# Earlier loads and transposes for the seventh pair, and third products spread one block per pass

## The chip, the cores and the metric

The kernel runs on one core of one Trainium2 chip. The metric is device time of one execution in microseconds (us). A profiled execution gives a span, from the first to the last instruction; it is usually 1.7 to 2.0 us shorter than the time. A single-core run is called slow when it is over 1.5% above the fastest of the same kernel; only fast runs are compared.

Engines in the profile: PE is TensorE (PEld its weight loads), DVE is VectorE, ACT is ScalarE, POOL is GpSimd, SP is SyncE. `L330` is line 330 of that run's own source, so line numbers shift a little between kernels.

## The reference, cut to what matters

```python
def reference(q, k, v, lam, moe_w_q, moe_w_k, moe_w_out):      # batch 4, 8 heads, 768 tokens, 64 columns
    x = linear_attention(q, k, v, lam)      # causal, decayed by lam per head, a running state per head
    x = x.transpose(0, 2, 1, 3).reshape(4, 768, 512)
    wq, wk = x @ w_q, x @ w_k               # 512 -> 64
    W = einsum('bsd,btd->bst', wq, wk) / 8
    mixed = einsum('bst,btd->bsd', W, x)
    return maximum(mixed, 0) @ w_out
```

The kernel uses that `W @ x` is `wq @ (wk.T @ x)`: a small product Y = wk.T x, then the "third products" Y.T wq (tile pm, evicted with Relu to rmT), then the output products with w_out (tile po).

## The kernel before

There are 16 pairs of heads (4 batches of 4 pairs) and one pass of the main loop for each, counted from 0. Pass n computes the scores of pair n, finishes pair n-1 and transposes q and k of pair n+1. Batch b's four pairs are complete about one pass after its last; the products for its 768 outputs are strewn over the passes of the next batch. The parts that matter, cut:

```python
    load_q(5); load_kv(5, "k"); load_wqk(); load_kv(5, "v")          # all on GpSimd's DMA queue
    nc.gpsimd.dma_start(out=wo, in_=moe_w_out...)                    # output weights, 512 KB in bf16
    pool = {0: ["q6", "s4", "k6", "v6"], 1: ["q7", "s5", "k7", "v7"], ...}   # s: scaling of v, on GpSimd
    for n in range(N):
        ...                                                          # GpSimd: what pool has for pass n
        outs      = {6: [(0, 0)], 9: [(0, 4)], 12: [(1, 0)], 13: [(1, 2)], 14: [(1, 3)], 15: [(1, 5)]}
        late_outs = {6: [(0, 1)], 7: [(0, 2)], 8: [(0, 3)], 10: [(0, 5)], 12: [(1, 1)], 14: [(1, 4)]}
        if n > 9 and n % 4 in (3, 0):
            mix_pm((n - 5) // 4, [0, 1] if n % 4 == 3 else [2, 3], engs=(nc.scalar, nc.vector) * 2)
        scores(n)
        inter(n - 1)                         # sums of states of pair n-1, times q
        masks(n, ((0, 0), (0, 1)))           # VectorE, PSUM -> SBUF
        back()                               # values(n-1), flip(n-2), mix_po for outs, in pass 9 and 13 mix_wk
        masks(n, ((1, 0),));  turn_q(n + 1)  # not in pass 5
        masks(n, ((1, 1),));  turn_k(n + 1)  # not in pass 5
        if n == 5: mix_wq(0); mix_py(0)
        states(n)
        for i, t in late_outs: mix_po(i, t)  # of pass n
        sums(n)
        if n == 5:
            mix_pm(0, [0, 1], ...); mix_pm(0, [2, 3], ...)
            turn(n + 1)
        if n in (9, 13): mix_wq(p); mix_py(p)
```

`mix_py` makes Y: twelve matmuls into PSUM, then three copies on ScalarE, all of which have to be done before the second matmul of a third-product block can start:

```python
        nc.scalar.copy(out=Y[:, 0, :], in_=py)
        for i in range(2):                                  # the same with its halves swapped
            nc.scalar.copy(out=Y[i * 64 : i * 64 + 64, 1, :], in_=py[o, :])
```

`mix_pm(b, [dd])` is one block: two matmuls of 384 columns and two evictions of 128x384, one on ScalarE and one on VectorE. The program hands out eight banks of PSUM (the memory that matmuls write to); a tile's bank is free when its eviction, the copy of it to SBUF, is done.

Of the kernel before, what the change touches and what calls it, by code (L numbers as in the profile page):

```python
# [28 lines left out]
def kernel(  # L29
# [11 lines left out]
    nc = tc.nc  # L41
# [16 lines left out]
    def pst(shape, dt, name):  # L58
        i = free.pop(0)
        t = ps.tile(shape, dt, tag=f"p{i}", name=name)  # L60
        held[id(t)] = (t, i)
        return t
# [5 lines left out]
    N = len(pairs)  # L68
# [4 lines left out]
    def q_rows(n):  # L73
        b, kk = pairs[n]
        return q[b, 2 * kk : 2 * kk + 2].rearrange("h (a p r) d -> p h a (r d)", p=128, r=2)

    def kv_rows(n, src):
        b, kk = pairs[n]
        return src[b, 2 * kk : 2 * kk + 2].rearrange("h (c p) d -> p h c d", p=128)

    def load_q(n):
        t = stage.tile([128, 2, 3, 2 * D], BF16, tag="fq", name="fq")
        nc.gpsimd.dma_start(out=t, in_=q_rows(n))  # L83
        staged[n, "q"] = t

    def load_kv(n, nm):
        t = stage.tile([128, 2, NCH, D], BF16, tag="f" + nm, name="f" + nm)
        nc.gpsimd.dma_start(out=t, in_=kv_rows(n, dict(k=k, v=v)[nm]))  # L88
        staged[n, nm] = t
# [137 lines left out]
    def turn(n):  # L227
        turn_q(n)
        turn_k(n)

    def turn_q(n):
        b, kk = pairs[n]
        fq = staged.pop((n, "q"))
        trq = pst([128, NCH, 2, 64], BF16, "trq")
        for a in range(3):
            for r in range(2):
                for hl in range(2):
                    nc.tensor.transpose(  # L238
                        trq[hl * 64 : hl * 64 + 64, 2 * a : 2 * a + 2, r, :],
                        fq[:, hl, a, r * D : (r + 1) * D],  # L240
                        ident,
                    )
        qT = tsb.tile([128, S], BF16, tag="qT", name="qT")
        nc.vector.tensor_tensor(  # L244
            out=qT,
            in0=trq.rearrange("d c r p -> d (c r p)"),
            in1=Dq[kk],
            op=ALU.mult,
        )
        done(trq)  # L250
        L[n]["qT"] = qT
# [75 lines left out]
    def masks(n, which):  # L327
        for a, hl in which:
            t = prb.tile([128, 3, CH], BF16, tag="pr", name="pr")
            nc.vector.tensor_tensor(out=t, in0=L[n]["sc"][a, hl], in1=maskc, op=ALU.mult)  # L330
            done(L[n]["sc"][a, hl])
            L[n]["pr"][a, hl] = t
# [83 lines left out]
    def mix_wq(b, kts=range(NP)):  # L416
        if 0 in kts:
            M[b]["wq"] = pst([128, HALF], F32, "wq")
        wq = M[b]["wq"]
        for kt in kts:  # L420
            for n in range(2):
                nc.tensor.matmul(  # L422
                    wq[n * 64 : n * 64 + 64, :],
                    wqk[:, 0, kt, :],
                    xT[b][:, kt, n * HALF : (n + 1) * HALF],
                    start=(kt == 0),
                    stop=(kt == NP - 1),
                    skip_group_check=True,
                )
        if NP - 1 in kts:  # L430
            wqT = hyp.tile([128, HALF], BF16, tag="wqT", name="wqT")
            nc.scalar.copy(
                out=wqT.rearrange("j (c p r) -> j c r p", c=3, r=2),
                in_=wq.rearrange("j (c r p) -> j c r p", c=3, r=2),
            )
            done(wq)
            M[b]["wqT"] = wqT
# [25 lines left out]
    def mix_pm(b, which, wide=True, engs=None):  # L463

        if isinstance(which[0], int):
            which = [(dd, n) for dd in which for n in range(2)]
        pms = [pst([128, HALF], F32, "pm") for _ in which]
        for m in range(1 if wide else 2):
            for (dd, n), pm in zip(which, pms):
                r = slice(n * 64, n * 64 + 64)  # L470
                c = (dd % 2) * CH
                if wide:
                    o, w = slice(0, 128), slice(c, c + CH)
                else:
                    o, w = slice(m * 64, m * 64 + 64), slice(c + m * 64, c + m * 64 + 64)
                nc.tensor.matmul(  # L476
                    pm[o, :],
                    M[b]["Y"][r, int(dd // 2 != n), w],
                    M[b]["wqT"][r, :],
                    start=True,  # L480
                    stop=True,
                    skip_group_check=True,
                )
        for i, ((dd, n), pm) in enumerate(zip(which, pms)):
            to = M[b]["rmT"][:, dd, n * HALF : (n + 1) * HALF]
            if engs and engs[i] is nc.vector:
                nc.vector.tensor_scalar(  # L487
                    out=to,
                    in0=pm,
                    scalar1=1.0 / 8.0,  # L490
                    scalar2=0.0,
                    op0=ALU.mult,
                    op1=ALU.max,
                )
            else:
                nc.scalar.activation(out=to, in_=pm, func=ACT.Relu, scale=1.0 / 8.0)  # L496
            done(pm)
# [10 lines left out]
    def mix_po(b, t, last=False):  # L508
# [39 lines left out]
    load_kv(5, "k")  # L548
    load_wqk()
    load_kv(5, "v")  # L550
    nc.gpsimd.dma_start(
        out=wo, in_=moe_w_out.rearrange("(kt p) (a j) -> p a kt j", p=128, j=CH)
    )


    pool = {
        0: ["q6", "s4", "k6", "v6"],
        1: ["q7", "s5", "k7", "v7"],
        2: ["q8", "k8", "s6", "v8"],
        3: ["q9", "s7", "k9", "v9"],  # L560
        4: ["q10", "s8", "k10", "v10"],
    }
    for n in range(N):
        b, kk = pairs[n]
        for what in pool.get(n, []):
            if what[0] == "s":
                scale_v(int(what[1:]), nc.gpsimd)
            elif what[0] == "q":
                load_q(int(what[1:]))
            else:  # L570
                load_kv(int(what[1:]), what[0])
        if 11 <= n + 5 < N:
            load_more(n + 5)
        if n + 5 >= N and n + 3 < N:
            scale_v(n + 3, nc.gpsimd)
        if n == 9:

            late = consts.tile([1, D], BF16, name="late")
            nc.sync.dma_start(out=late, in_=staged[14, "v"][0:1, 0, 0, :])
            store()  # L580
        p = b - 1
        outs = {
            6: [(0, 0)],
            9: [(0, 4)],
            12: [(1, 0)],
            13: [(1, 2)],
            14: [(1, 3)],
            15: [(1, 5)],
        }.get(n, [])

        late_outs = {
            6: [(0, 1)],
            7: [(0, 2)],
            8: [(0, 3)],
            10: [(0, 5)],
            12: [(1, 1)],
            14: [(1, 4)],
        }.get(n, [])

        def back():  # L600

            if kk == 1 and n > 8:
                flip(n - 2, nc.scalar)
            if n >= 1:
                values(n - 1)
            if n >= 2 and not (kk == 1 and n > 8) and n != 5:
                flip(n - 2, nc.scalar if n < 5 else None)
            for i, t in outs:
                mix_po(i, t)
            if kk == 1 and n > 8:  # L610
                mix_wk(p)


        if n > 9 and n % 4 in (3, 0):
            mix_pm(
                (n - 5) // 4,
                [0, 1] if n % 4 == 3 else [2, 3],
                engs=(nc.scalar, nc.vector) * 2,
            )
        scores(n)  # L620
        if n >= 1:
            inter(n - 1)
        masks(n, ((0, 0), (0, 1)))
        back()

        if 1 <= n < 3:
            make_dq(n + 1)
        if n in (2, 3):
            scale_v(n, nc.vector)
        masks(n, ((1, 0),))  # L630
        if n < N - 1 and n != 5:
            turn_q(n + 1)
        masks(n, ((1, 1),))
        if n < N - 1 and n != 5:
            turn_k(n + 1)
        if n == 5:

            mix_wq(p)
            mix_py(p)
        states(n)  # L640
        if n == 4:
            flip(n - 1)
        for i, t in late_outs:
            mix_po(i, t)
        sums(n)
        if n == 0:
            scale_v(1, nc.vector)
        if n == 4:
            mix_wk(p, (0, 1, 2))
            mix_wk(p, (3,))  # L650
        if n == 5:
            for dds in ([0, 1], [2, 3]):
                mix_pm(0, dds, engs=(nc.scalar, nc.vector) * 2)
            turn(n + 1)
        if kk == 1 and n > 8:
            mix_wq(p)
            mix_py(p)
# [53 lines left out]
```

## Time and profile before

| | before |
|---|---|
| time, median of 4 runs | 99.84 us (99.44 to 100.2) |
| span of the profiled run | 97.8 us |
| scores of passes 5, 6, 9, 10, 13, 14 start at | 27.59, 34.20, 46.00, 51.44, 64.22, 69.65 us |
| last inter products (pair 15) start at | 78.08 us |

### The profile page before, as it was taken

The page shows a single profiled execution, that of the slowest core. Times are in us where ns is not written, and L with a number is a line of the kernel's source. Part 1 is how long each engine was busy: PE and PEld are TensorE (multiplying, and loading weights), DVE is VectorE, ACT ScalarE, POOL GpSimd, SP SyncE. Part 2 cuts the span into 40 slices and gives each one's busy share as a digit, 9 for nine tenths or more (in the row PEclk, how much of TensorE's full clock was granted, in tenths as well). Part 3 has the DMA queues.
Part 4 walks back from the last instruction along what each step waited for, and adds up shares of the span by engine and source line. Part 5 has one row for each costly group of instructions (what it writes and reads, how often), then busy time and mean ns, then how long its engine had stood idle before and what let it go on. Part 6 is the DMA issues. An engine that isn't in the chain of part 4 may idle for free.

```text
span 97.8 us, 3522 instructions
## 1 busy us (share of the span) xinstructions
PE 84.5 (86%) x1507; PEld 56.7 (58%) x1507; DVE 71.0 (73%) x156; ACT 62.0 (63%) x118; POOL 66.7 (68%) x69
## 2 busy tenths in 40 slices
PE   4997578598997599999999997999999999999940
PEld 1344466377875376866788475668865466433420
DVE  6648978799685986998389999974989971283520
ACT  5084477976939846664768864667977746677230
POOL 5999999999999598999999999998050000000000
PEclk9999999999999999999999999999999999999999
DMA  0999999999999999999999999999999224325583
GB/s 9 220 160 157 167 165 160 166 165 158 171 184 156 166 168 158 158 146 130 139 160 163 131 151 133 128 156 187 290 401 371 97 107 184 137 111 210 215 316 113
DMA packets 68976, 16.79 MB, mean 172 GB/s; under 512 B 65762, under 2 KB 66018, under 8 KB 68962
## 3 DMA queue, kind: packets, MB, share of 16 engines
q0 software_dynamic: 63776, 9.90, 139.0%
q1 hardware_dynamic: 5042, 6.56, 18.7%
q8 instruction: 11, 0.18, 0.7%
q10 hardware_dynamic: 144, 0.13, 0.4%
q14 instruction: 3, 0.02, 0.1%
HBM read 20.19 MB, written 6.29 MB: 271 GB/s over the span
## 4 chain that ended last, share of the span: by engine, by line
PE 36%; POOL 29%; DMA 13%; DVE 12%; issue 3%; ACT 3%; POOLq 0%
PE po L515 16%; DMA fv<-in_v_dram 8%; POOL fv L88 7%; POOL fk L88 7%; POOL fq L83 6%; DMA fk<-in_k_dram 6%; DVE pr L330 5%; POOL vn L212 4%; PE xp L379 3%; PE oa L359 3%; DVE rmT L487 2%; PE wk L402 2%; PE py L443 2%; PE wq L422 2%; PE trk L258 2%
## 5 line engine op out<-in xcount | busy, mean ns | idle before, releaser
L330 DVE TENSOR_TENSOR pr<-sc,maskc 128x384 bf16<-128x384 f32 x64 | 33.3, 550 | 2.1 <-PE sc L317 1.8
L515 PE MATMUL po<-wo,rmT 128*128 128x512 bf16 (+1 forms) x100 | 24.0, 372 | 0.0
L212 POOL TENSOR_TENSOR vn<-fv,DvI 128x768 bf16<-128x768 bf16 x12 | 18.2, 1514 | 4.1 <-PE oa L359 2.7
L371 ACT CAST xnat<-oa 128x384 bf16<-128x384 f32 x31 | 13.4, 483 | 8.7 <-PE oa L359 8.7
L527 ACT COPY osb<-po 128x512 f32<-128x512 f32 (+1 forms) x22 | 12.6, 579 | 9.7 <-PE po L515 9.7
L262 ACT COPY kT<-trk 128x768 bf16<-128x768 bf16 x16 | 12.8, 799 | 7.3 <-PE trk L258 7.2
L88 POOL DMA_DIRECT2D fv<-in_v_dram x16 | 17.1, 1069 | 0.0
L88 POOL DMA_DIRECT2D fk<-in_k_dram x15 | 16.1, 1075 | 0.0
L83 POOL DMA_DIRECT2D fq<-in_q_dram x16 | 14.2, 885 | 0.8 <-POOLq L695 0.8
L515 PEld LDWEIGHTS <-rmT 128*128 128x128 bf16 x100 | 8.5, 98 | 8.4 <-issue 0.8
L317 PE MATMUL sc<-qT,kT 64*128 64x128 bf16 x192 | 8.9, 218 | 4.2 <-ACT kT L262 2.4
L244 DVE TENSOR_TENSOR qT<-trq,dq 128x768 bf16<-128x768 bf16 x16 | 8.8, 553 | 4.2 <-PE trq L238 2.7
L317 PEld LDWEIGHTS <-kT 64*128 64x128 bf16 x192 | 5.9, 94 | 8.6 <-ACT kT L262 6.5
L258 PE MATMUL trk<-ident,fk 128*64 128x128 bf16 x180 | 7.7, 221 | 2.3 <-DMA fk<-in_k_dram 2.2
L238 PE MATMUL trq<-ident,fq 128*64 128x128 bf16 x192 | 8.5, 224 | 0.2 <-DMA fq<-in_q_dram 0.2
L487 DVE TENSOR_SCALAR rmT<-pm 128x384 bf16<-128x384 f32 x16 | 8.1, 550 | 0.6 <-PE pm L476 0.6
L359 PE MATMUL oa<-vn,pr 128*128 128x64 bf16 x192 | 8.4, 194 | 0.0
L379 PE MATMUL xp<-ident,xnat 128*128 128x128 bf16 x96 | 8.0, 220 | 0.2
L238 PEld LDWEIGHTS <-fq 128*64 128x64 bf16 x192 | 5.9, 110 | 3.3 <-issue 2.0
L277 PE MATMUL dps<-vn,fk 128*64 128x128 bf16 (+4 forms) x150 | 7.6, 232 | 0.1
L258 PEld LDWEIGHTS <-fk 128*64 128x64 bf16 x180 | 5.7, 110 | 3.3 <-DMA fk<-in_k_dram 3.3
L496 ACT ACTIVATE rmT<-pm 128x384 bf16<-128x384 f32 x16 | 7.0, 496 | 0.1
(62 smaller groups left out, 112.7 us busy)
## 6 DMA issues: line engine op xcount, KB each, us to landing
out_dram<-osb SPq DMA_DIRECT2D x23, 256.0 KB, 2.7
fq<-in_q_dram POOLq DMA_DIRECT2D x16, 192.0 KB, 5.7
fv<-in_v_dram POOLq DMA_DIRECT2D x16, 192.0 KB, 5.7
fk<-in_k_dram POOLq DMA_DIRECT2D x15, 192.0 KB, 6.0
wo<-in_moe_w_out_dram POOLq DMA_DIRECT2D x1, 512.0 KB, 9.4
k<-in_k_dram SPq DMA_DIRECT2D x1, 384.0 KB, 3.7
out_dram<-osb ACTq DMA_DIRECT2D x1, 128.0 KB, 2.1
out_dram<-osb SPq DMA_DIRECT2D x1, 128.0 KB, 2.1
```

Of the source, the lines that this page charges most:

```text
L83: nc.gpsimd.dma_start(out=t, in_=q_rows(n))
L88: nc.gpsimd.dma_start(out=t, in_=kv_rows(n, dict(k=k, v=v)[nm]))
L212: eng.tensor_tensor(out=vn, in0=fv, in1=DvI[:, 2 * kk : 2 * kk + 2, :].unsqueeze(3).to_broadcast([128, 2, NCH, D]), op=ALU.mult,)
L238: nc.tensor.transpose(trq[hl * 64 : hl * 64 + 64, 2 * a : 2 * a + 2, r, :], fq[:, hl, a, r * D : (r + 1) * D], ident,)
L258: nc.tensor.transpose(trk[hl * 64 : hl * 64 + 64, c * CH : (c + 1) * CH], kn[:, hl, c, :], ident)
L262: nc.scalar.copy(out=kT, in_=trk)
L317: nc.tensor.matmul(sc[a, hl][:, cc, :], kT[r, c * CH : (c + 1) * CH], qchunk(n, r, c), start=True, stop=True, skip_group_check=True,)
L330: nc.vector.tensor_tensor(out=t, in0=L[n]["sc"][a, hl], in1=maskc, op=ALU.mult)
L359: nc.tensor.matmul(oa[hl][:, c, :], pr[c // 3, hl][:, c % 3, :], vn[:, hl, c, :], start=False, stop=(c == NCH - 1), skip_group_check=True,)
L371: nc.scalar.copy(out=to, in_=oa[hl])
L515: nc.tensor.matmul(po, M[b]["rmT"][:, kt, t * CH : (t + 1) * CH], wo[:, c // CH : (c + w) // CH, kt, :], start=(kt == 0), stop=(kt == 3),)
L527: nc.scalar.copy(out=osb[:, c : c + w], in_=po.rearrange("p a j -> p (a j)"))
```

## The change

It wants to fill the hole of pass 5 by transposing pair 6 before the third products of batch 0, which needs q and k of pair 6 to be loaded ahead of the output weights. It also spreads the third products of batches 0, 1 and 2 over the passes, one block of a batch at a time, ahead of the scores, so that VectorE never has four evictions or two at once to do. As the blocks end later, the output products move to later passes. The last batch's third products stay where they are. The diff, cut to its core:

```diff
     load_kv(5, "v")
+    load_q(6)
+    load_kv(6, "k")
     nc.gpsimd.dma_start(out=wo, ...)
-        0: ["q6", "s4", "k6", "v6"],
+        0: ["s4", "v6"],
+    thirds = {7: [(0, 2)], 8: [(0, 3)], 10: [(1, 0)], 11: [(1, 1)], 12: [(1, 2)],
+              13: [(1, 3)], 14: [(2, 0)], 15: [(2, 1)]}
-        outs:      6: [(0, 0)], 9: [(0, 4)], 12: [(1, 0)], 13: [(1, 2)], 14: [(1, 3)], 15: [(1, 5)]
+        outs:      8: [(0, 0)], 10: [(0, 3)], 13: [(1, 0)], 14: [(1, 2)], 15: [(1, 4)]
-        late_outs: 6: [(0, 1)], 7: [(0, 2)], 8: [(0, 3)], 10: [(0, 5)], 12: [(1, 1)], 14: [(1, 4)]
+        late_outs: 8: [(0, 1)], 9: [(0, 2)], 10: [(0, 4)], 12: [(0, 5)], 13: [(1, 1)], 14: [(1, 3)], 15: [(1, 5)]
-        if n > 9 and n % 4 in (3, 0):
-            mix_pm((n - 5) // 4, [0, 1] if n % 4 == 3 else [2, 3], engs=(nc.scalar, nc.vector) * 2)
+        for i, dd in thirds.get(n, []):
+            mix_pm(i, [dd], engs=(nc.scalar, nc.vector))
         scores(n)
...
-        if n < N - 1 and n != 5:
+        if n < N - 1:
             turn_q(n + 1)
+        if n == 5:
+            mix_wq(p)
         masks(n, ((1, 1),))
-        if n < N - 1 and n != 5:
+        if n < N - 1:
             turn_k(n + 1)
         if n == 5:
-            mix_wq(p)
             mix_py(p)
...
         if n == 5:
-            for dds in ([0, 1], [2, 3]):
-                mix_pm(0, dds, engs=(nc.scalar, nc.vector) * 2)
-            turn(n + 1)
+            mix_pm(0, [0, 1], engs=(nc.scalar, nc.vector) * 2)
```

More of the change, by code (lines that the diff above doesn't have):

```diff
@@ L561 @@
         4: ["q10", "s8", "k10", "v10"],
+    }
+    thirds = {
+        7: [(0, 2)],
+        8: [(0, 3)],
+        10: [(1, 0)],
+        11: [(1, 1)],
+        12: [(1, 2)],
+        13: [(1, 3)],
+        14: [(2, 0)],
+        15: [(2, 1)],
     }
@@ L582 @@
         outs = {
-            6: [(0, 0)],
-            9: [(0, 4)],
-            12: [(1, 0)],
-            13: [(1, 2)],
+            8: [(0, 0)],
+            10: [(0, 3)],
+            13: [(1, 0)],
+            14: [(1, 2)],
+            15: [(1, 4)],
+        }.get(n, [])
+        late_outs = {
+            8: [(0, 1)],
+            9: [(0, 2)],
+            10: [(0, 4)],
+            12: [(0, 5)],
+            13: [(1, 1)],
             14: [(1, 3)],
             15: [(1, 5)],
-        }.get(n, [])
-        late_outs = {
-            6: [(0, 1)],
-            7: [(0, 2)],
-            8: [(0, 3)],
-            10: [(0, 5)],
-            12: [(1, 1)],
-            14: [(1, 4)],
         }.get(n, [])
@@ L611, in back @@
                 mix_wk(p)
-        if n > 9 and n % 4 in (3, 0):
-            mix_pm(
-                (n - 5) // 4,
-                [0, 1] if n % 4 == 3 else [2, 3],
-                engs=(nc.scalar, nc.vector) * 2,
-            )
+        for i, dd in thirds.get(n, []):
+            mix_pm(i, [dd], engs=(nc.scalar, nc.vector))
         scores(n)
```

## The prediction

> **What bounds the kernel now.** One core, 99.59 us; the profiled execution spans 97.8 us, so about 1.8 us lie outside the span and I take them as constant. Passes of the main loop are counted from 0 as in the code: pass n scores pair n and transposes q and k of pair n+1. I read the page's busy shares first.
>
> ```profile
> PE 84.5 (86%) x1507; PEld 56.7 (58%) x1507; DVE 71.0 (73%) x156; ACT 62.0 (63%) x118; POOL 66.7 (68%) x69
> ```
>
> No engine is full over the span, so the limit changes by stage and an average decides nothing. Next the chain of waits in order of time (start, length, what):
>
> ```profile
> 27.01 1.50 POOL vn L212
> 28.51 0.98 POOL fk L88
> 29.49 7.49 DMA fv<-in_v_dram
> 36.98 0.07 issue
> 37.05 0.33 POOL vn L212
> ...
> 38.47 5.65 DMA fk<-in_k_dram
> 44.12 0.04 issue
> 44.16 0.53 PE trk L258 x12
> 44.69 0.41 PE dps L277 x10
> 45.10 0.98 PE po L515 x4
> ```
>
> The reader is to see that until 44.12 us the end is set by the loads alone: GpSimd issues, v of pair 7 lands at 36.98, its scaling on GpSimd follows, only then is k of pair 9 issued, and it lands at 44.12. TensorE enters the chain there. From then on the chain is TensorE, with VectorE between 52.9 and 60.3 and again between 74.3 and 78.0.
>
> Then the timeline of PE (start, length, line, operation) around the places where the change acts:
>
> ```profile
> 29.30 0.82 PE L443 MATMUL py<-xnat,wkn 128*64 128x256 bf16 x12
> 29.96 0.58 PE L277 MATMUL dps<-vn,fk 128*64 128x320 bf16 x10
> 30.59 0.33 PE L476 MATMUL pm<-wqT,Y 64*128 64x384 bf16 x1
> 31.36 0.82 PE L476 MATMUL pm<-wqT,Y 64*128 64x384 bf16 x7 [0.43 <-ACT Y L458]
> 32.11 0.53 PE L238 MATMUL trq<-ident,fq 128*64 128x128 bf16 x12
> 32.65 0.53 PE L258 MATMUL trk<-ident,fk 128*64 128x128 bf16 x12
> 34.20 0.51 PE L317 MATMUL sc<-qT,kT 64*128 64x128 bf16 x12 [1.03 <-DVE qT L244]
> ...
> 50.68 0.82 PE L443 MATMUL py<-xnat,wkn 128*64 128x256 bf16 x12
> 51.44 0.51 PE L317 MATMUL sc<-qT,kT 64*128 64x128 bf16 x12
> ```
>
> Two readings. Pass 5 has a hole: third products (pm) wait for Y, the pair-6 transposes stand behind them, and scores of pass 6 start at 34.20 after 1.03 us idle. And a pm placed right after py cannot start: py starts at 29.30, the pm that needs all of Y at 31.36, 2.06 us later. In pass 9 py starts at 50.68 and scores follow 0.76 us later, because there the pm comes one pass later. ACT's timeline has the cause, three copies one after the other:
>
> ```profile
> 51.55 0.37 ACT L452 CAST Y<-py 128x256 bf16<-128x256 f32 x1
> 51.93 0.74 ACT L458 CAST Y<-py 64x256 bf16<-64x256 f32 x2
> ```
>
> Y is complete at 52.67, 1.99 us after py began.
>
> **What the Trainium skill says.** (1) "PSUM — Partial Sum Buffer", section "Engine vs sequencer instructions": matmuls start and complete in program order. The trace agrees: q of pair 6 landed at 31.28, but its transposes ran at 32.11, behind the waiting pm. So a waiting pm ahead of scores holds the scores. (2) "TensorE: Matmul & The Clock Gate", "Back-to-back issue gap": N/2.4 + 2.5 ns, 216 ns for 512 columns. The chain has a four-matmul output product (po) at 0.86 us, 215 ns each: agrees; 0.97 us where the chain counts the last one's drain. (3) "DMA: Bandwidth & Descriptors", "Anatomy of one DMA": about 2.0 us plus bytes/436e3, 2.45 us for 192 KB. The trace differs: k of pair 9, with a short queue, took 5.65 us; I use that. (4) "Perfetto Trace Analysis", "Optimization Strategy": the most contended engine can change over time; the trace agrees, as above.
>
> **The change part by part.** Nothing is added or removed: same matmuls, evictions and transfers, in another order.
>
> *Loads.* Issues were v5, wo, q6, scaling of v4, k6, v6; they become v5, q6, k6, wo, scaling, v6. Landings of the trace: v5 26.92, wo 29.75 (2.83 later), q6 31.28, k6 32.60, v6 33.37. At about 1.3 us each q6 should land near 28.3, k6 near 29.6, wo near 32.4; v6 and all after it as before, since the sum of work ahead is the same. Hence v7 at 36.98 and k9 at 44.12 stay: neither waits for TensorE. The scaling of v4 ends about 1.2 us later, near 25.3, still before its use at 25.63.
>
> *Pass 5.* Pair 6's q is turned from 28.63 (0.46), wq 0.67, k turned near 29.75 (0.36), py from 30.15, dps, four pm at about 32.3, scores of pass 6 near 32.7: 1.5 us earlier than 34.20.
>
> *Passes 6 to 8.* Before, four po ran here, after only two (passes 6 and 7 have none). But transposes need k7 (35.84), k8 (39.68) and k9 (44.12). Pass 7's scores come near 37.1 (before 38.62), pass 8's near 40.95 (before 42.17), and in pass 8 the k transposes wait for k9 until 44.12 (before: same). Then dps and one po as before: scores of pass 9 at about 46.0, before 46.00. The gain is zero there, and two po (0.86 + 0.97 = 1.83 us of TensorE) that before were done are still to do.
>
> *Pass 9.* First-factor products (wk) come straight after values instead of behind a po, so they stall on ACT's copy of the last transpose (ends 48.08), and end near 48.7 (before 49.1): -0.35. One late po: +0.97. Then pm(1,0) right after py: scores at py + 2.2 instead of + 0.76: +1.45. Scores of pass 10: 51.44 + 2.1 = 53.5.
>
> *Passes 10 to 12.* Pass 10 gets two po instead of one, +0.86, less two pm: pass 11 starts at 58.0 against 55.18, +2.8. Passes 11 and 12 were bound by VectorE, with two evictions of pm (0.47 each) at the head of each: before 55.40 to 59.71, 4.31 each. With one, 3.85 each, from 58.1: 62.0 and 65.85. The state sums that end there release the inter products of pass 13, at 66.0 against 64.56: +1.4. So about 1.4 us come back, 0.9 of it the two evictions moved into TensorE-bound passes, the rest gaps that VectorE had before in pass 12. po that filled this VectorE-bound stretch (two in pass 12, now one) went to passes where TensorE sets the pace.
>
> *Pass 13.* Two po instead of one, +0.97; pm(2,0) behind py again, +1.45: scores of pass 14 at 73.5 against 69.65, +3.85.
>
> *Passes 14 and 15.* Pass 14: two fewer pm, -0.15. Pass 15: before, 74.26 to 78.08 was set by VectorE with about 0.35 us of slack on TensorE; with a second po (0.9) TensorE sets it, +0.55. At the last inter products: 78.08 + 4.25.
>
> *Tail.* From there the code is the same, 19.6 us.
>
> Check by another sum: 1.83 (two po behind the k9 gate) + 2 x 1.27 (idle for Y) + 0.4 (wk stall) - 0.5 (balance of VectorE relief and lost filling) = 4.3 us. I chose 4.0, since a hand-made sum forgets small slack more often than it invents it: 99.6 + 4.0 = 103.6 us.
>
> **The rivals.** (a) *The hole of pass 5 is worth its whole size*: 1.5 us are gained and stay, giving 98.1 us. For it: the hole is real, 1.03 us idle plus the Y wait. Against it: the chain runs through v7, its scaling and k9 at that time, not through TensorE. (b) *Levelling wins*: one VectorE eviction per pass instead of two relieves passes 11 and 12, and po moved there costs nothing; with the Y wait hidden the sum would be 4.25 - 2.9 = +1.3 us, 100.9 us, or even 99.6 if the two po also fell into slack. For it: VectorE is the chain in 52.9 to 60.3. Against: py to complete Y is 1.99 us both times it can be read, and nothing stands between py and pm in the new order. (c) *The loads shift*: if q6 and k6 ahead of wo let GpSimd run ahead and k9 lands 0.5 us earlier, all gains 0.5 us: 103.1; if wo or a full set of eight outstanding loads holds GpSimd up, k9 lands later and it is 104 or more. The trace shows eight completion semaphores in turn on GpSimd's loads, and k6 would have to wait for 21.31 and wo for 22.37, within 0.2 us of when they would be issued anyway.
>
> **Range and chances.** Low end 102.0: half of the Y stall or one of the two po is absorbed and k9 is a little early. High end 104.8: no relief in passes 11 and 12. Within 2% means below 101.6 us; that needs both Y stalls hidden, which I give 0.09. Faster by over 2% needs rival (a) and more: 0.02. Slower by over 2%: 0.89.
>
> **What would show it.** Right: scores of pass 6 near 32.7; k9's landing still near 44.1 with TensorE idle before it in passes 6 to 8; scores of pass 9 near 46.0; a wait of PE on ACT's Y of about 1.2 us in passes 9 to 10 and 13 to 14; VectorE no longer taking two evictions of pm together in passes 11 and 12; a tail of 19.6 us. Wrong: k9 clearly before 43.5; scores of pass 9 before 45; no wait of pm on Y; or passes 10 to 12 shorter than 11.5 us from scores to scores.

## More of the kernel before

The busy shares of the whole span, the chain of waits and the timeline around the changed places are shown in the prediction. What they don't show is how full each engine is stage by stage. The following view of the kernel before gives the busy time of each engine in stretches: pass 5, passes 6 to 8, pass 9, passes 10 to 12, pass 13, passes 14 to the last inter products, and the tail. Columns: stretch, its length, then busy us (and instructions) of PE, PEld, DVE, ACT, POOL, the granted clock, DMA share and GB/s.

```profile
27.59:34.20 6.61, 5.08 (x99) 3.71 (x97) 5.32 (x11) 5.05 (x11) 5.52 (x6) 1.00 2.15 168
34.20:46.00 11.80, 11.71 (x238) 8.29 (x237) 10.21 (x21) 6.73 (x12) 11.52 (x12) 1.00 2.09 153
46.00:51.44 5.44, 5.36 (x124) 4.41 (x124) 3.28 (x10) 3.98 (x7) 5.44 (x6) 1.00 2.08 149
51.44:64.22 12.78, 11.90 (x245) 8.09 (x244) 12.41 (x33) 8.85 (x19) 12.78 (x13) 1.00 1.94 141
64.22:69.65 5.43, 5.34 (x123) 4.40 (x123) 3.43 (x10) 3.98 (x7) 3.76 (x3) 1.00 1.89 180
69.65:78.08 8.43, 8.07 (x146) 5.08 (x144) 7.70 (x21) 6.57 (x15) 1.47 (x1) 1.00 0.84 309
78.08:97.78 19.70, 15.84 (x138) 8.08 (x138) 7.68 (x16) 9.48 (x20) 0.00 (x0) 1.00 0.46 173
```

TensorE has a hole of 1.53 us in pass 5 (6.61 less 5.08). In passes 6 to 8 it is full (11.71 of 11.80), and GpSimd nearly so (11.52). In passes 9 and 13 TensorE is full again (5.36 of 5.44 and 5.34 of 5.43), with VectorE and ScalarE far from it. In passes 10 to 12 VectorE is (12.41 of 12.78), with 0.88 us to spare on TensorE. GpSimd is busy nearly without a break from pass 6 to pass 12, but with loads and scalings of later pairs.

## The result, and the profile after

The changed kernel takes 103.78 us (103.63 to 103.99, 4 runs) against 99.84 us: slower by 4.0%, ratio 1.0398 with a 95% interval of 1.0346 to 1.0449. A ratio here is the mean time of one kernel's fast runs over that of the other's of the same rounds, so it is not quite the ratio of the medians. Run again later beside other experiments it took 103.86 us, ratio 1.0413 (1.0387 to 1.0439). Results are correct in every run told of here.

The same stretches in the changed kernel:

```profile
27.50:33.10 5.60, 4.32 (x95) 3.42 (x93) 3.37 (x7) 3.43 (x8) 5.10 (x5) 1.00 2.02 174
33.10:45.80 12.70, 10.94 (x238) 8.07 (x235) 11.87 (x26) 7.07 (x14) 12.07 (x12) 1.00 2.11 153
45.80:53.39 7.59, 6.14 (x125) 4.52 (x125) 3.57 (x9) 5.26 (x11) 7.59 (x7) 1.00 2.08 152
53.39:65.53 12.14, 11.57 (x242) 8.18 (x243) 11.35 (x28) 7.46 (x15) 12.14 (x13) 1.00 1.93 139
65.53:73.58 8.05, 7.03 (x130) 4.96 (x127) 4.50 (x13) 6.08 (x13) 3.76 (x4) 1.00 1.42 261
73.58:82.33 8.75, 8.68 (x148) 5.49 (x149) 7.60 (x19) 5.36 (x11) 0.21 (x1) 1.00 0.32 122
82.33:101.83 19.50, 15.66 (x140) 7.96 (x136) 7.57 (x15) 10.01 (x21) 0.00 (x0) 0.98 0.49 186
```

Line by line against the view of before: -1.01 in pass 5, +0.90 in passes 6 to 8, +2.15 in pass 9, -0.64 in passes 10 to 12, +2.62 in pass 13, +0.32 in passes 14 and 15, -0.20 in the tail. With -0.09 ahead of pass 5 that is +4.05, the whole difference of the spans (101.8 less 97.8). Two passes carry more than all of it.

What the two passes lose is seen in the changed kernel's chain of waits (start, length, what), the part of pass 9:

```profile
49.76 0.97 PE po L515 x4
50.72 0.77 PE wq L422 x8
51.49 0.67 PE py L443 x12
52.17 0.02 issue
52.19 0.37 ACT Y L452
52.56 0.03 issue
52.59 0.37 ACT Y L458
52.97 0.37 ACT Y L458
53.34 0.05 issue
53.39 0.23 PE pm L476
```

The chain leaves TensorE at 52.17 and comes back at 53.39: three copies on ScalarE, and in that time TensorE can do only the first matmul of the pm, because the scores behind the second one are next in its order. The timeline of PE in the changed kernel shows the same from its side:

```profile
47.22 0.25 PE L402 MATMUL wk<-wqk,xT 128*128 128x64 bf16 x3
47.92 0.79 PE L402 MATMUL wk<-wqk,xT 128*128 128x64 bf16 x21 [0.45 <-ACT xT L385]
...
51.33 0.82 PE L443 MATMUL py<-xnat,wkn 128*64 128x256 bf16 x12
52.62 0.33 PE L476 MATMUL pm<-wqT,Y 64*128 64x384 bf16 x1 [0.47 <-ACT Y L452]
53.39 0.33 PE L476 MATMUL pm<-wqT,Y 64*128 64x384 bf16 x1 [0.44 <-ACT Y L458]
53.39 0.55 PE L317 MATMUL sc<-qT,kT 64*128 64x128 bf16 x10
```

py starts at 51.33 and the scores at 53.39, 2.06 us later; before it was 0.76 us, 1.30 less. In pass 13 it is the same: py at 71.52, scores at 73.58. The wk line shows a second, smaller loss: before, an output product stood ahead of wk and covered ScalarE's copy of the last transpose; now wk stops after three matmuls and waits 0.45 us.

Passes 6 to 8 show a third. There TensorE has two output products (1.83 us) less to do and two third-product blocks more (0.77 us less in sum), yet the stretch grew from 11.80 to 12.70 us, and TensorE is idle for 1.76 us of it. The timeline of PE in the changed kernel names waits on k of pairs 7 and 8:

```profile
35.93 0.53 PE L258 MATMUL trk<-ident,fk 128*64 128x128 bf16 x12 [0.47 <-DMA fk<-in_k_dram]
37.40 0.51 PE L317 MATMUL sc<-qT,kT 64*128 64x128 bf16 x12 [0.27 <-ACT kT L262]
39.90 0.53 PE L258 MATMUL trk<-ident,fk 128*64 128x128 bf16 x12 [0.60 <-DVE pr L330]
41.38 0.51 PE L317 MATMUL sc<-qT,kT 64*128 64x128 bf16 x12 [0.27 <-ACT kT L262]
```

The third line's releaser reads "DVE pr", but the matmul's weight load at the same time waited for the landing of k of pair 8, at 39.86; a wait for several semaphores is put down to the one that came last, and VectorE's pr ended 0.05 us after that landing. So VectorE is a close second here: with the evictions of third products it is busy for 4.11 of the 4.30 us of pass 6 and 3.86 of the 3.98 us of pass 7, and the chain of waits of this run goes through it from 33.31 to 39.92, while that of the same kernel run again (e11) goes through k of pair 8, landed at 39.88. e6, below, shows what is left when the loads come earlier.

So scores of pass 9 start at 45.80 instead of 46.00: of the 1.1 us that scores of pass 6 were early 0.2 is left, and two output products more are still to do.

### The profile page after: what moved, and what is told of

Same layout as the page of the kernel before. It is cut to its first block, busy times and chain, and to the rows that moved or that the text cites. A ratio compares the mean times of both kernels' runs of the same rounds, so it can differ in the third digit from the quotient of the medians.

```text
span 101.8 us, 3520 instructions
## 1 busy us (share of the span) xinstructions
PE 85.5 (84%) x1507; PEld 57.3 (56%) x1507; DVE 70.7 (69%) x156; ACT 62.1 (61%) x118; POOL 66.8 (66%) x69
## 3 DMA queue, kind: packets, MB, share of 16 engines
HBM read 20.19 MB, written 6.29 MB: 260 GB/s over the span
## 4 chain that ended last, share of the span: by engine, by line
PE 52%; POOL 15%; DVE 11%; DMA 8%; ACT 7%; issue 3%; POOLq 0%; DVEq 0%; ACTq 0%
PE po L515 22%; DMA fk<-in_k_dram 8%; POOL fv L88 5%; DVE pr L330 5%; POOL fq L83 5%; POOL fk L88 4%; PE xp L379 4%; PE oa L359 3%; PE trk L258 3%; PE trq L238 3%; PE py L443 3%; PE wq L422 3%; PE pm L476 3%; PE dps L277 3%; PE wk L402 2%
## 5 line engine op out<-in xcount | busy, mean ns | idle before, releaser
L476 PE MATMUL pm<-wqT,Y 64*128 64x384 bf16 x32 | 5.8, 331 | 2.3 <-ACT Y L458 1.3
```

## The experiments

My theory: (1) the wait on Y, twice, directly; (2) two output products that leave a stretch held by loads and are paid in passes where TensorE sets the pace; (3) some relief of VectorE in passes 10 to 12 against it. Rivals: the hole of pass 5 is worth its size; levelling VectorE wins by itself; the wait on Y would be hidden anyway.

### The first block behind the scores: e2 and e12, beside e11

Only the place of the first block of batches 1 and 2 changes, against the changed kernel:

```diff
-        for i, dd in thirds.get(n, []):
-            mix_pm(i, [dd], engs=(nc.scalar, nc.vector))
+        if n not in (10, 14):
+            for i, dd in thirds.get(n, []):
+                mix_pm(i, [dd], engs=(nc.scalar, nc.vector))
         scores(n)
...
         back()
+        if n in (10, 14):
+            for i, dd in thirds.get(n, []):
+                mix_pm(i, [dd], engs=(nc.scalar, nc.vector))
```

> The changed kernel, but in passes 10 and 14 the first third-product block comes behind scores, inter products and values instead of ahead of the scores; same work. My theory: both waits on Y (1.27 us each of idle TensorE) go, scores of pass 10 follow py by about 0.8 us; -2.2 to -2.6 us against the changed kernel, so +1.4 us against before (101.3). Rival (the loss is all from output products that were moved to later passes, the Y wait would be hidden by VectorE's work otherwise): within 0.5 us of the changed kernel (+3.5 to +4).

It took 102.15 us (101.73 to 104.64), ratio 1.0245 (1.0177 to 1.0313): the rival falls, but the interval is wide, and the clock of the profiled run was 0.992. From scores of pass 9 to the last inter products, the trace was 2.3 us shorter than the changed kernel's, as expected; passes 6 to 8 were 0.6 us later there. So it was run again, beside the changed kernel on the same chip:

> The changed kernel again, unchanged, beside the next run on one chip: +3.9 us against before. It also shows whether v of pair 7 lands at 37.0 as in its first profile, or at 38 to 38.6 as in four of five other runs with the new load order.

> The run with the first block behind the scores again: its first trace had the passes 9 to 15 2.3 us shorter than the changed kernel, as expected, but passes 6 to 8 0.6 us later. My theory: 2.2 to 2.6 us faster than the changed kernel on the same chip. Rival: under 1.2 us faster.

The changed kernel took 103.86 us again, the one with the block behind the scores 101.36 us (101.19 to 101.55), ratio 1.0161 (1.0136 to 1.0187) to before. The same work in another order is 2.50 us faster. The timeline of PE in e12:

```profile
51.34 0.82 PE L443 MATMUL py<-xnat,wkn 128*64 128x256 bf16 x12
52.09 0.51 PE L317 MATMUL sc<-qT,kT 64*128 64x128 bf16 x12
...
54.34 0.34 PE L476 MATMUL pm<-wqT,Y 64*128 64x384 bf16 x2
```

py is where it was (51.34), the scores follow after 0.75 us, and when pm comes 2 us later Y is there. So the wait on Y is 2.5 us of the 4.

e12 also shows where the rest lies. Against the kernel before, its pass 9 is 0.85 us longer (45.80 to 52.09) and its pass 13 1.31 (64.42 to 71.16, where TensorE has a second output product); passes 14 and 15 are 0.43 longer, passes 10 to 12 0.45 shorter, and the tail 0.22 shorter. The changed kernel's +2.15 and +2.62 are these two figures with 1.30 us for the wait added to each. So what is left is paid in passes 9 and 13, where TensorE sets the pace: pass 13 has one output product more, and pass 9 has as many as before, but the one it has no longer covers ScalarE's copy ahead of wk.

The other question of e11, v of pair 7: it landed at 37.5 in e11 and 37.2 in e12, against 36.98 in the first trace and 38.0 to 38.6 in e1, e2 and e3. It varies from run to run with the same code, and does not explain the result.

### An output product in the wait: e3

The late output product of passes 9 and 13 goes behind py, in the changed kernel:

```diff
-        for i, t in late_outs:
-            mix_po(i, t)
+        if n not in (9, 13):
+            for i, t in late_outs:
+                mix_po(i, t)
         sums(n)
...
         if kk == 1 and n > 8:
             mix_wq(p)
             mix_py(p)
+            for i, t in late_outs:
+                mix_po(i, t)
```

> The changed kernel, but the late output product of passes 9 and 13 is issued behind py instead of ahead of wq, so that 0.97 us of TensorE work lies in each wait for Y; nothing else moved. My theory: scores of pass 10 and 14 come 0.97 us earlier each; -1.9 us against the changed kernel, +2.0 against before (101.8). Rival (the wait on Y costs nothing): no change, +3.9 against before.

It took 102.65 us (102.05 to 103.72), ratio 1.029 (1.0201 to 1.0379): between theory and changed kernel, with a wide interval. The spread lies outside the program's instructions: all three fast runs span 100.2 us, 1.6 less than the changed kernel, while their times go from 102.05 to 103.2. The timeline of PE in e3 is clear:

```profile
50.63 0.82 PE L443 MATMUL py<-xnat,wkn 128*64 128x256 bf16 x12
51.38 1.04 PE L515 MATMUL po<-wo,rmT 128*128 128x512 bf16 x4
52.35 0.67 PE L476 MATMUL pm<-wqT,Y 64*128 64x384 bf16 x2
52.69 0.55 PE L317 MATMUL sc<-qT,kT 64*128 64x128 bf16 x10
```

From py to scores it is still 2.06 us, but 0.97 us of it is now work that was to be done anyway. Pass 9 took 6.50 us instead of 7.59, pass 13 6.96 instead of 8.05: 1.1 us less each. The wait is as long as before, and work that doesn't need Y can be put into it.

### Only the spreading: e4

The kernel before, with nothing but this:

```diff
+    thirds = {10: [(1, 0)], 11: [(1, 1)], 12: [(1, 2), (1, 3)], 14: [(2, 0)], 15: [(2, 1)]}
-        if n > 9 and n % 4 in (3, 0):
-            mix_pm((n - 5) // 4, [0, 1] if n % 4 == 3 else [2, 3], engs=(nc.scalar, nc.vector) * 2)
+        for i, dd in thirds.get(n, []):
+            mix_pm(i, [dd], engs=(nc.scalar, nc.vector))
         scores(n)
```

> The kernel before with only the third products of batches 1 and 2 spread one block per pass ahead of the scores (passes 10, 11, 12 twice, 14, 15); loads, pass 5 and all output products as before. My theory: two waits on Y of 1.27 us, less 0.8 us of relief on VectorE in passes 11 and 15: +1.8 us against before (101.6). Rival (levelling wins): -0.9 us (98.9).

It took 102.7 us (101.32 to 103.39), ratio 1.0238 (1.0122 to 1.0353). The rival "levelling wins" falls. Its stretches (pass 9, passes 10 to 12, pass 13, passes 14 and 15):

```profile
46.00:52.80 6.80, 5.81 (x126) 4.53 (x127) 3.89 (x10) 5.19 (x11) 6.80 (x7) 1.00 2.06 151
52.80:65.40 12.60, 11.77 (x243) 8.20 (x245) 12.07 (x31) 7.75 (x15) 12.60 (x12) 1.00 1.93 138
65.40:72.10 6.70, 5.71 (x126) 4.45 (x125) 3.69 (x10) 5.17 (x11) 3.62 (x4) 1.00 1.54 242
72.10:80.28 8.18, 7.87 (x144) 5.08 (x145) 7.39 (x19) 5.50 (x11) 0.59 (x1) 1.00 0.59 222
```

Passes 9 and 13 are 1.36 and 1.27 us longer than before. The relief I gave VectorE, 0.8 us, came to 0.18 in passes 10 to 12 and 0.25 in 14 and 15. My reading: in passes 10 to 12 the block only moved from one pass that VectorE sets to another, and their sum is what counts.

### Only batch 0: e5

Batch 0's loads, early transposes, third products and late output products as in the changed kernel, with (0, 5) in pass 11; batches 1 and 2 as before.

```diff
 # against the changed kernel
-        10: [(1, 0)], 11: [(1, 1)], 12: [(1, 2)], 13: [(1, 3)], 14: [(2, 0)], 15: [(2, 1)],    # of thirds
+        # and the mix_pm of passes 11, 12 and 15 ahead of the scores, as in the kernel before
-        outs:      8: [(0, 0)], 10: [(0, 3)], 13: [(1, 0)], 14: [(1, 2)], 15: [(1, 4)]
+        outs:      8: [(0, 0)], 10: [(0, 3)], 12: [(1, 0)], 13: [(1, 2)], 14: [(1, 3)], 15: [(1, 5)]
-        late_outs: 8: [(0, 1)], 9: [(0, 2)], 10: [(0, 4)], 12: [(0, 5)], 13: [(1, 1)], 14: [(1, 3)], 15: [(1, 5)]
+        late_outs: 8: [(0, 1)], 9: [(0, 2)], 10: [(0, 4)], 11: [(0, 5)], 12: [(1, 1)], 14: [(1, 4)]
```

> Batch 0 as in the changed kernel (loads, early transposes, third products in passes 5, 7 and 8, output products of batch 0 in passes 8 to 11), batches 1 and 2 as in the kernel before. My theory: scores of pass 9 at about 46 in both, no wait on Y later; pass 9 about 0.25 us shorter, pass 10 0.86 us longer for its second output product, the one in pass 11 free because VectorE sets that pass: +0.6 us against before (100.2). Rival (each output product put off past pass 9 costs its full length, as the sum in my prediction had it): +1.8 (101.4).

It took 101.34 us (100.87 to 102.45), ratio of the fast runs 1.0131 (1.008 to 1.0182): +1.3%, between the two. Its profile fell in the slow state, so no line of it is read. My expectation had a slip: it counted pass 9 as 0.25 us shorter and forgot the late output product that comes in (0.97). e12, which has no wait on Y, shows pass 9 at 6.29 us (45.80 to 52.09) against 5.44 before, +0.85. The output product that left pass 9 saved next to nothing, since wk then waits for ScalarE; the one that came in cost its length. With +0.85 in pass 9 and 4.59 against 3.74 us in pass 10 (scores to scores in the changed kernel and before, at 53.39 and 57.98, 51.44 and 55.18) less what passes 5 to 8 gain, 1.3 is about what to expect: the two sum to 1.7, and 0.2 is gained by scores of pass 9. So passes 9 and 10 account for the loss without the output product of pass 11; that it was free, as my theory had it, fits but is not shown. The spans agree with the times: 99.1 to 99.2 us in the three fast runs, against 97.7 to 98.1 in the fast runs of the kernel before.

### Only the early transposes: e1 and e10

e1 is the kernel before with the first, third and last parts of the diff above, but all of batch 0's third products at the end of pass 5, and all output products where they were:

```diff
+    load_q(6)
+    load_kv(6, "k")                        # ahead of wo; turn_q(6), mix_wq, turn_k(6), mix_py as in the change
             for dds in ([0, 1], [2, 3]):
                 mix_pm(0, dds, engs=(nc.scalar, nc.vector) * 2)
-            turn(n + 1)
```

> The kernel before with only the load order and the early transposes of pair 6 (all third products and output products where they were). My theory: scores of pass 6 about 0.7 us earlier than 34.2, but the landings of k of pairs 8 and 9 (39.7 and about 44) and the scaling behind v of pair 7 take it back; time between -0.8 and 0 us against before, most likely -0.3 (99.5). Rival (the hole of pass 5 is worth its size): -1.5 us (98.3).

It took 100.04 us (99.57 to 100.62), ratio 1.005 (0.9985 to 1.0115): no gain, so the rival falls. But my reason was not the one that the trace shows. The timeline of PE in e1:

```profile
30.20 0.60 PE L443 MATMUL py<-xnat,wkn 128*64 128x256 bf16 x8
31.53 0.41 PE L443 MATMUL py<-xnat,wkn 128*64 128x256 bf16 x4 [0.72 <-issue]
...
33.17 0.82 PE L476 MATMUL pm<-wqT,Y 64*128 64x384 bf16 x7 [0.44 <-ACT Y L458]
33.68 0.21 PE L317 MATMUL sc<-qT,kT 64*128 64x128 bf16 x1
34.15 0.79 PE L317 MATMUL sc<-qT,kT 64*128 64x128 bf16 x11 [0.16 <-DVE rmT L487]
```

No load is waited for. There is a new stop of 0.72 us after the eighth py matmul, in which TensorE waits for nothing that the profile shows; the wait on Y is still there; and the scores wait for VectorE's eviction of a third product (rmT), that is, for a PSUM bank. Moving the transposes forward took one wait out of pass 5 and let others take its place.

e10 takes the PSUM banks out of it: the second half of batch 0's third products goes behind the values of pass 6.

```diff
 # against e1
-            for dds in ([0, 1], [2, 3]):
-                mix_pm(0, dds, engs=(nc.scalar, nc.vector) * 2)
+            mix_pm(0, [0, 1], engs=(nc.scalar, nc.vector) * 2)
...
         back()
+        if n == 6:
+            mix_pm(0, [2, 3], engs=(nc.scalar, nc.vector) * 2)
-        outs: 6: [(0, 0)]      late_outs: 6: [(0, 1)]
+        late_outs: 6: [(0, 0), (0, 1)]
```

> The early-turn run with the second half of batch 0's third products moved from the end of pass 5 to behind the values of pass 6, both output products of pass 6 at its end. In the early-turn run the scores of pass 6 waited on evictions of pm. If those evictions were all that ate the gain: scores of pass 6 complete at about 33.6, -0.5 us against before (99.2). If the loads and TensorE's work in passes 6 to 8 set the time whatever pass 5 does: 0 (-0.2 to +0.4).

It took 99.56 us (99.38 to 100.08), ratio 0.999 (0.9963 to 1.0016): the same as before. Scores of pass 6 start at 33.10, 1.1 us earlier than before, but pass 9's at 45.87. Its stretches, pass 5 and passes 6 to 8:

```profile
27.60:33.10 5.50, 4.32 (x94) 3.42 (x93) 3.36 (x7) 3.42 (x8) 5.08 (x5) 1.00 2.02 174
33.10:45.87 12.77, 12.59 (x246) 8.78 (x243) 11.66 (x26) 8.24 (x16) 11.26 (x11) 1.00 2.00 147
```

TensorE is idle for 1.18 us in pass 5 (5.50 less 4.32), not much less than the 1.53 us before. So the hole was not filled, only its cause replaced: what made pass 5 shorter is the half of the third products that moved into pass 6. And passes 6 to 8 are as full as before, so what moves there is paid there.

### The output weights later still: e6

In the changed kernel, wo is loaded behind k of pair 8:

```diff
-    nc.gpsimd.dma_start(out=wo, ...)            # ahead of the loop
-        2: ["q8", "k8", "s6", "v8"],
+        2: ["q8", "k8", "wo", "s6", "v8"],
```

> The changed kernel with the load of the output weights put off behind k of pair 8, so that all loads of pairs 6 to 8 land 2 to 3 us earlier. My prediction's theory (the landings hold passes 6 to 8): scores of pass 9 at about 44.6 instead of 45.8, -1.2 us against the changed kernel, +2.7 against before. Rival (with one or two evictions of pm in each of the passes 6 to 8, VectorE holds them at 3.9 us each anyway): scores of pass 9 at about 45.4, -0.4 us, +3.5 against before.

The time was unsteady, 103.95 to 108.77 us, two of four runs slow and no ratio given; the profile is of a fast run. Both expectations missed: scores of pass 9 started at 46.08. Passes 6 and 7 did get faster, 3.64 and 3.67 us (scores at 32.53, 36.17, 39.84) instead of 4.30 and 3.98, now with VectorE without a gap from 32.73 on: the loads had cost about 1 us there, and VectorE is the next limit. Then k of pair 9 stopped TensorE. The timeline of PE and, below it, of POOL in e6:

```profile
42.85 0.53 PE L238 MATMUL trq<-ident,fq 128*64 128x128 bf16 x12 [0.24 <-DMA fq<-in_q_dram]
44.24 0.53 PE L258 MATMUL trk<-ident,fk 128*64 128x128 bf16 x12 [0.86 <-DMA fk<-in_k_dram]
```

```profile
35.97 1.20 POOL L83 DMA_DIRECT2D fq<-in_q_dram  x1
36.80 1.86 POOL L212 TENSOR_TENSOR vn<-fv,DvI 128x768 bf16<-128x768 bf16 x1
38.23 1.40 POOL L88 DMA_DIRECT2D fk<-in_k_dram  x1
```

v of pair 7 landed at 35.54, 1.4 us earlier than in the changed kernel, and still k of pair 9 was issued at 38.23 (38.47 in the changed kernel) and landed at 44.19. GpSimd works without a gap from 27.0 to 41.4: each issue takes it about 1 us and each scaling 1.5 us. In the changed kernel GpSimd stands idle in this place, 0.88 us for v of pair 6 and 0.26 for v of pair 7; here the issue of the output weights, moved into the list at 32.33, fills the same time. So e6 did not test what an earlier v of pair 7 alone would do: it took out one gate and put in another.

The other traces do tell. In both kernels and in e1, e2, e3, e11 and e12, k of pair 9 is issued 1.49 or 1.50 us after v of pair 7 lands, early (36.98 and 38.47) or late (38.58 and 40.07, e2). So this landing does gate the issue, as the prediction had it; what an earlier landing can gain in the two kernels is small, because GpSimd would be free only 0.28 and 0.26 us earlier (its idle time before the scaling). But the issue hardly moves the landing: issued anywhere between 38.23 (e6) and 40.07, k of pair 9 landed between 43.18 (e11) and 44.19 (e6), and only in e6 did TensorE lose time to it.

### Relieving VectorE by ScalarE: e7 and e8

If VectorE sets passes 10 to 12 of the kernel before, its evictions of pm on ScalarE should gain there, without any new order. e7 puts all four of passes 11, 12 and 15 on ScalarE, e8 three of four:

```diff
-                engs=(nc.scalar, nc.vector) * 2,
+                engs=(nc.scalar,) * 4,                                     # e7
+                engs=(nc.scalar, nc.vector, nc.scalar, nc.scalar),         # e8
```

> The kernel before, with all four evictions of pm of passes 11, 12 and 15 on ScalarE (two of four were on VectorE); order as before. My theory (VectorE set passes 11, 12 and 15 of the kernel before, so relief there is real, only the changed kernel pays for it with the wait on Y): VectorE loses 0.93 us a pass, TensorE takes over; passes 10 to 12 about 1.0 us shorter, pass 15 0.3; -1.0 us against before (98.6). Rival (ScalarE's 1.76 us of evictions at the head of the pass delay its copies and give it back): 0 or slower.

> As the run before it, but three evictions on ScalarE and one on VectorE. My theory: VectorE loses 0.47 us a pass: -0.6 us against before (99.0). Rival: 0 or slower.

e7 took 99.89 us, ratio 1.0009 (0.998 to 1.0038); e8 99.53 us, ratio 0.9985 (0.9939 to 1.0032). My theory falls for e7; the 0.6 us that it gave e8 is at the very edge of the interval. The timeline of PE and of DVE in e7, pass 11:

```profile
56.37 0.30 PE L341 MATMUL oa<-gs,qT 64*128 64x64 bf16 x9 [0.20 <-ACT rmT L496]
```

```profile
55.55 1.02 DVE L330 TENSOR_TENSOR pr<-sc,maskc 128x384 bf16<-128x384 f32 x2
57.50 0.56 DVE L387 COPY xT<-xp 128x768 bf16<-128x768 bf16 x1 [0.93 <-PE xp L379]
```

The inter products wait for an eviction by ScalarE (rmT), which now has four of them and frees the PSUM bank later, and VectorE, now with less to do, idles 0.93 us for the transposes behind them. Which engine is fullest in a stretch did not tell which relief would shorten it.

### The change without its two faults: e9

Early loads and transposes, batch 0's third products half in pass 5 and half ahead of the scores of pass 7, three output products by pass 9, the sixth in pass 11, batches 1 and 2 as before:

```diff
 # against e1
-            for dds in ([0, 1], [2, 3]):
-                mix_pm(0, dds, engs=(nc.scalar, nc.vector) * 2)
+            mix_pm(0, [0, 1], engs=(nc.scalar, nc.vector) * 2)
+        if n == 7:
+            mix_pm(0, [2, 3], engs=(nc.scalar, nc.vector) * 2)             # ahead of the scores
-        outs: 6: [(0, 0)], 9: [(0, 4)]                late_outs: 6: [(0, 1)], 7: [(0, 2)], 8: [(0, 3)], 10: [(0, 5)]
+        outs: 7: [(0, 0)], 8: [(0, 1)], 9: [(0, 3)]   late_outs: 8: [(0, 2)], 10: [(0, 4)], 11: [(0, 5)]
```

> Loads and early transposes of pair 6 as changed; batch 0's third products half in pass 5, half ahead of the scores of pass 7; its output products in passes 7, 8 (two), 9, 10 and 11, three of them by scores of pass 9; batches 1 and 2 as in the kernel before. No pm stands directly behind its py, and the sixth output product lies in pass 11, which VectorE sets. My theory: the loads still hold scores of pass 9 at about 46.0, and the rest is as before: 0 us against before (-0.4 to +0.5). Rival (the hole of pass 5 is worth something once no eviction and no output product stands in its way): -0.8 us (98.9).

It took 100.02 us (99.65 to 100.96), ratio 1.0037 (1.0001 to 1.0073): within what my theory said for the time, and the rival falls. Its reason was off: scores of pass 9 came at 46.65, not 46.0, though k of pair 9 had landed at 43.57 and was first used at 44.83, so it was not this load that held them. No version here is shown faster than the kernel before.

## Why the prediction was right

It said 103.6 us (102.0 to 104.8), and 103.78 us were measured; slower by over 2% had the chance 0.89.

- *Pass 5 gains 1.5 us, scores of pass 6 at 32.7.* Mis-sized: 33.10, a gain of 1.1. The stop of 0.79 us in py was not foreseen. In e6, which has no such stop, it was 32.53.
- *The gain is gone by pass 9, scores at about 46.0.* Right in the time, 45.80, and e1, e10 and e9 gain nothing either. Of the mechanism, the waits for k of pairs 7 and 8 were right, if sized a little short: scores of passes 7 and 8 came at 37.40 and 41.38 instead of 37.1 and 40.95, with VectorE close behind, which the prediction did not count as a limit here. The last gate was wrong: TensorE was to wait for k of pair 9 until 44.12, but it landed at 43.61 and was not waited for, because TensorE, later than forecast, had only then come to it. That the two errors cancel is luck. When the same kernel ran again (e11), k of pair 9 landed at 43.18, before the 43.5 that the prediction named as a sign of being wrong, with the same time. That v of pair 7 gates the issue of k of pair 9 was right (38.47 again). The prediction also read the chain of waits as if TensorE were slack until 44.12; the stretches show it full from 34.2 on, together with GpSimd.
- *Pass 9: -0.35 for wk, +0.97, +1.45; scores of pass 10 at 53.5.* Measured 53.39, with trq at 48.64 where the prediction had the end of wk at 48.7. e12 and e11 give both waits on Y as 2.50 us together; the prediction's check had 2 x 1.27.
- *Passes 10 to 12 give 1.4 us back.* The predicted starts were met: 58.0 for pass 11 (57.98), 66.0 for the inter products of pass 13 (66.10), so 1.3 came back. As to why, it is argued and not shown. e4 has one of the two moved evictions without the moved output products, and where 0.47 us of relief was forecast for it, its passes 10 to 12 are 0.18 us shorter. How the rest splits between the second eviction and the output product that left pass 12 no run separates.
- *Pass 13 and on.* Scores of pass 14 at 73.5 (73.58), last inter products at 78.08 + 4.25 = 82.33 (82.33), tail 19.6 us (19.50). At that point the sum of the parts, 4.25, was met exactly. The 0.25 us taken off it for caution then matched a tail that is 0.20 shorter and was not forecast: that the total of 4.0 came so close to 4.05 is luck at this last step.
- *Its readings of the skill.* The second leaves out that the same section calls this formula the isolated gap and gives about 131 ns for 512 columns in a stream with weight loads; the 215 ns of the trace fit the formula and not that. The third calls the queue short; three earlier loads were in flight when k of pair 9 was issued (they landed at 39.68, 40.62 and 41.83), so the 5.65 us are no measure of one DMA alone.
- *Rivals.* (a) falls by e1, e9 and e10, (b) by e4 and e2/e12, (c) by the changed kernel itself: k of pair 9 landed 0.51 us earlier (0.94 in e11), as (c) supposed, though GpSimd did not run ahead, and neither run was faster for it.

What stays open: whether the stop in py is an instruction fetch (see the last section); how much of the two displaced output products each later pass paid, since e5's time lies between the two expectations and its profile is not usable; why e6 is unsteady. Untried is a shorter wait on Y, with its copies shared between two engines.

## What to carry to other kernels

An instruction in an in-order queue costs not its own length but the time until its operand is ready, so a product that waits for another engine belongs behind work that doesn't need it; the same matmuls behind the scores instead of ahead were worth 2.50 us. Filler has a place: taken out of a spot where it covered another engine's latency and put where its engine is already full, it costs about its whole length (0.85 us in pass 9, 1.31 in pass 13). And a hole in a busy engine is worth something only if nothing else stands right behind it and the stages that follow are not already full: here pass 5 could be made 1.1 us shorter with no gain at all.

## What the Trainium skill lacked or had wrong

- "DMA: Bandwidth & Descriptors", "Anatomy of one DMA": it gives about 2.0 us plus bytes/436e3 for a DMA issued from GpSimd, 2.45 us for 192 KB (an estimate from that page), and in that section nothing for a load with others in flight. Here, with several in flight nearly always, the quickest load of 192 KB in the kernel before took 3.6 us and the medians of q, k and v are 5.7, 6.0 and 5.7 us. No run has one load alone, so the formula itself is not tested.
- "Runtime: NRT & Kernel Launch", "Instruction fetch mechanics": it says that instructions are fetched in blocks of 256 and that crossing a block is mostly hidden. Nine of the ten traces with the early transposes have a stop of 0.34 to 0.81 us after the eighth py matmul, with nothing awaited in the profile. In all nine, by the trace's DMA records, a 16 KB transfer on the profile's "instruction" queue began 2.28 to 2.50 us before the stop ended (changed kernel: 28.98 and 31.28). In e6, which has no stop, it began about 1 us earlier, at 27.98. So a fetch that came too late fits all ten; no run moved it on purpose, and it is not shown.
- "Perfetto Trace Analysis", "Optimization Strategy": it says that bubbles can mean too little PSUM for the next tile. What it lacks is that the bank can be held by another engine's eviction of another tile, so that relief of the fullest engine only moves the wait: in e1 scores waited for VectorE's eviction and in e7 inter products for ScalarE's, 0.16 and 0.20 us, and e7's relief of VectorE came to nothing (ratio 1.0009).
